# Decay by one power on GpSimd, a first mask from factor and triangle, stripe 1 on the whole array, and a new order of the list

## The chip, the cores and the metric

The kernel runs on one core of a Trainium2 chip. The core has five engines that run side by side and wait for one another by semaphores: TensorE (PE in the profile; its weight loads are PEld), VectorE (DVE), ScalarE (ACT), GpSimd (POOL) and SyncE (SP, which here only issues DMAs). Matmuls write to PSUM, eight banks of 128 partitions x 2 KB; everything else lies in SBUF. The metric is the device time of one execution in microseconds (us).

## The reference

Decayed linear attention over blocks of 64 positions (batch 4, 8 heads, 768 positions, head size 64), then an MLP with a quadratic, clipped activation. One block of the attention, for each batch and head:

```python
Dmask = np.where(rel >= 0, lam ** rel, 0.0)          # rel = i - j inside a block
intra = (q_b @ k_b.T * Dmask) @ v_b
inter = (q_b * lam ** (pos + 1)) @ kv_state
out_b = intra + inter
kv_state = lam ** 64 * kv_state + (k_b * lam ** (63 - pos)).T @ v_b
```

The outputs of all heads are laid side by side as x (3072 tokens x 512) and go through

```python
h = x @ w_in                                          # 512 -> 2048
g = where(h >= 1, h, where(h <= -1, 0, (h + 1) ** 2 / 4))
out = g @ w_out                                       # 2048 -> 512
```

## The kernel before, in words

The kernel works with blocks of 128 positions. The 24 blocks of the four batches are cut into eight stripes (`STRIPES`): stripe 0 has four blocks of batch 0, stripe 1 the two that are left of it, stripes 2 to 7 three each. A unit is a stripe and a pair of heads; stripe s has units s0 to s3. The MLP then runs on a whole stripe.

All order is written out by hand: `ORDER` is a list of words, each of which issues the instructions of one step, and every engine runs its own instructions in that order. The words of the attention, for unit 00 as an example: `L00k`, `L00q`, `L00v` load heads (SP issues them); `k00a`, `q02g`, `v01d` cast one to bf16, k and q times a power of lam, on ScalarE (a), VectorE (d) or GpSimd (g) (lines 275 to 311); `T00`, `Q00` transpose k and q on TensorE (334), `t00`, `u00` copy the transposes out on ScalarE (342, 344); `S00` is the scores (362), `s00` the mask on VectorE (371); `R00` the products k.T v (416, 422), `r00` the running state on VectorE (435, 444); `O00` the output (472 to 504), `o00` its copy into x on ScalarE (516). `z` spreads a cast k with zeros between the heads, for the form "f" (393, 395). Of the MLP: `K` is a part of the first three tiles of the up product for one quarter of x (575), `P` a whole tile of it (561), `h` its relu on ScalarE (584), `A` the rest of the activation on VectorE (541 to 543), `Y` a quarter of a down product (593), `y` its copy (601), `U` its store. `W0` to `W3` load quarters of w_in, `W4` to `W7` of w_out, as DMAs issued by GpSimd (232, 236); a word with `@` waits until the load named behind it has landed. `D1`, `D2` are one or two matmuls of a unit matrix whose result nobody reads (549, "warm-ups" below). `B` builds the masks of a pair of heads (216), `E` fills lam_z, the factors of stripe 0's scan (207), `J` zeroes the middle parts of the v and z tiles (260), `G` of other tiles.

`FORMS` says how each stripe's products of two heads stand in TensorE's array. "p": each head's 64 rows or columns in a half of its own, two matmuls side by side. "f": the whole array, with one head's data and zeros for the other, the state as a 128x128 block with zero corners. "w": outputs by token, transposes by DMA.

The powers of lam are made once: iota on GpSimd gives positions, ScalarE takes Ln(lam) (191), VectorE multiplies (194), ScalarE takes Exp (197); all later casts read `dec`. PSUM: four banks turn over for the MLP and the warm-ups (`pmm`), two for transposes, states and outputs (`pat`), two hold scores.

Of the kernel before, what the change touches and what calls it, by code (L numbers as in the profile page):

```python
# [23 lines left out]

FORMS = "ppffwwww"
STRIPES = [(0, 0, 4), (0, 4, 2), (1, 0, 3), (1, 3, 3), (2, 0, 3), (2, 3, 3), (3, 0, 3), (3, 3, 3)]

ORDER = """
L00k D1 D1 L01q D2 D2 D1 L02q L01k q01d k00a k01d D1 T00 q02g L00q q00d L01v L02k D1 D2 T01 t00
Q00 Q01 k02d v01a D1 B0a u00 S00 T02 D2 D1 B3a u01 L00v Q02 t01 L02v D2 E s00 S01 D2 L03q v02g
v00a L03k u02 D2 W0 D1 R00 q03g B1a L03v W2 D2 D2 B2a s01 W1@L00v L11q t02 W3 R01 r00 S02 r01
O00 v03g O01 o00 k03d D1 o01 T03 s02 L10v@W2 W4@L10v J Q03 t03 u03 R02 r02 S03 R03 O02 o02 D2
r03 s03 K00 L10q@W1 K02 O03 W5@L02k q11g K01 q12d q10g o03 K03 h02 P03 L10k@W2 h01 P08 q13g L11k
L11v k11g P0b h03 W6@L02q h00 P06 h08 h06 h0b P07 P04 P05 P09 W7@L00k h07 P0a Q12 h09 A00 Q10
k13d L20k@W5 h05 P0f h0a h04 k12d P0d u10 k10a P0e v13g T10 t10 T12 t12 P0c L20q u12 S10 L21k@W6
h0e D2 v10a h0f T11 T13 L20v Q13 A01 h0c Q11 Y030 u13 A02 s10 Y020 h0d t13 Y000 u11 Y010 t11  # L40
Y011 R10 v12a v11a r10 R11 S11 Y031 Y021 s11 Y001 S12 r11 R13 q21g O10 o10 Y022 Y032 A03 r13 s12
Y033 S13 R12 O11 Y012 y03 s13 r12 k20a o11 O13 k21a O12 q20d Y023 L21v@W1 o13 o12 z20a v21d P10
v20g y02 T20 T21 Q20 h10 P19 t21 P18 k23d Y002 L21q@W5 v22d Y013 q22g z21a t20 u20 h18 R20 P11
S20 k22d y01 h19 Q21 P13 h11 P12 u21 L31k q23d P16 L30k z22a Y003 T22 h13 h12 U02 P17 P15 L31q
h16 t22 r20 s20 y00 h17 A10 S21 Q22 k32d s21 P1a u22 Q23 T23 h1a R21 r21 L30q u23 P14 L30v v23g
z23g P1c P1f h15 k33g q30g P1d h14 P1b q31g S22 h1f h1c L31v O20 L40k t23 R23 k31a A11 o20 h1d
s22 P1e Y100 R22 Y110 k30a r23 z31g v32g r22 Y111 S23 O21 h1b L40q h1e Q30 T30 A12 s23 o21 A13
L40v Y101 u30 t30 O22 z30g T31 z32a o22 Y112 O23 v31d G40 v30g Y102 Q31 o23 S30 P22 s30 G42 R31
v33g u31 q32d t31 h22 P23 R30 Y113 P21 r30 h23 R32 G41 P29 q33d z33a y11 h21 r31 T32 Q32 P20 r32
k40d t32 u32 R33 r33 P2b h29 S31 P27 O30 q40g U03 h20 s31 h2b o30 S32 q42g Y103 Q33 T33 s32 t33  # L50
O31 P25 G43 h27 L50k u33 o31 T40 P26 P24 h26 h24 O32 S33 A20 P2c v40d q41d s33 h25 h2c U01 y10
k42a P2a O33 P28 o32 h28 k43g v41g P2d P2f T42 A21 P2e o33 k41d h2a q43d h2d G50 h2e R40 P32 P31
h2f R41 S40 A22 r41 h32 v42a P30 T41 A23 s40 P33 h31 h30 h33 Y200 P34 Y201 P36 L50v P37 T43 Y202
Y203 k51a L50q U11 L60k h37 h36 y20 P35 v43a P3a h3a r40 S41 O40 h34 A30 s41 P39 o40 v51d h39
R42 k50a P3b r42 P38 O41 U10 S42 P3f h35 h38 o41 P3e s42 q50a h3f X40 h3e O42 P3c q52d o42 A31
R43 v50d P3d h3b S43 r43 T50 q51d h3c Y210 Y220 v52g Y211 h3d k52a s43 Y212 R51 A32 X41 L60q
Y300 Y320 O43 Y321 U00 A33 Y322 X42 Y213 o43 X43 S50 y21 Y221 T51 Y301 Y323 y32 Y302 Y303 T52
P41 P40 R52 s50 r51 S51 R50 y30 P42 L60v Y222 q60a k53a k61d Y223 q53a q62g r50 h42 q61g k60g
s51 T53 h41 P43 h43 h40 P4b S52 T60 r52 U21 Y310 P46 h46 Y311 h4b s52 O52 P44 k62g O50 v61g o52
A40 h44 v53d k63g q63g v62a O51 U20 P48 T62 P4d Y312 S53 y22 T61 o50 h4d h48 v60a o51 P4c P49  # L60
h4c P47 R60 U30 s53 S60 h49 h47 s60 Y313 X50 L70k R53 r60 P45 S61 h45 y31 P4f X52 L70q O60 v63a
o60 P4a P4e X51 h4f h4a r53 Y410 Y400 A41 O53 o53 q71g Y420 h4e A42 Y411 R61 A43 U32 Y421 Y401
Y412 Y402 R62 X53 s61 Y413 P57 k72a Y403 h57 T63 L70v k70g r61 r62 y41 P51 h51 P5a S62 s62 P50
O61 y40 v73d Y422 R63 P53 k73a h50 o61 h53 S63 h5a s63 k71g q70g P52 U40 v72d P58 Y423 T71 O62
h52 y42 P59 P54 h59 h54 T70 P56 h56 P5b r63 P55 O63 A50 S70 h55 o62 o63 q73d s70 P5d R73 P5f h58
r73 R72 U41 X61 U22 P5e h5d h5b h5f v70a h5e U31 X62 P5c Y500 X63 A51 X60 A52 Y510 R70 h5c Y501
S71 Y511 P60 P63 h63 Y512 h60 Y502 A53 P68 q72g T73 r72 s71 Y503 Y513 P62 h68 v71g h62 T72 P61
y51 h61 S72 P67 R71 P6a P65 h67 h6a s72 r70 P6b h6b P66 U51 O72 y50 P69 A60 S73 r71 P6f o72 s73
h66 P64 X72 O71 h6f h69 P6d Y520 o71 Y521 h6d O70 P6c A62 o70 X71 h64 O73 Y522 h65 h6c P6e Y523
Y610 Y600 A61 o73 h6e A63 y52 X70 Y611 Y612 U42 Y601 Y602 X73 P75 Y613 Y603 y61 P78 P70 y60 h78  # L70
h75 P76 h76 P7b h7b P73 Y620 P71 U50 h73 h70 P72 U52 P7a U61 h71 P79 Y621 h72 h7a h79 Y622 A72
Y623 P74 h74 y62 P77 P7e h77 h7e P7d P7f A70 P7c h7d h7f h7c U60 Y710 A71 Y700 Y711 Y701 Y712
U62 A73 Y713 Y702 Y703 y71 y70 U71 U70 Z72
"""


# [5 lines left out]
def kernel(  # L82
# [64 lines left out]
    def load(s, n, which):  # L147
# [39 lines left out]
    one = const.tile([128, 1], F32, name="one")  # L187
    nc.vector.memset(one, 1.0)

    ln_lam = const.tile([128, H], F32, name="ln_lam")  # L190
    nc.scalar.activation(out=ln_lam, in_=lam_b, func=AF.Ln)
# [5 lines left out]
    nc.scalar.activation(out=dec, in_=ex, func=AF.Exp)
# [168 lines left out]
    def att_mask(u):  # L366

        s, hp = u
        C, T = shape(s)[:2]
        d = st[u]  # L370
        nc.vector.tensor_tensor(  # L371
            out=d["sc"][:, :, 0:C, :],
            in0=d["ps"][:, :, 0:T].rearrange("p h (c i) -> p h c i", c=C),
            in1=_ins(mask[:, 2 * hp:2 * hp + 2, :], 2, C), op=AX.mult)

    def before(u):

        s, hp = u
        C, T, first, last, fm = shape(s)
        if first:  # L380
            return None
        ss = st[s - 1, hp]["ss"]
        return ss[:, :, CM - 1] if s == 1 else ss[:, shape(s - 1)[0] - 1, :]

    def att_z(u, eng):
# [8 lines left out]
        else:  # L394
            (nc.gpsimd if eng == "g" else nc.vector).tensor_copy(dst, src)

    def att_r(u):

        s, hp = u
# [51 lines left out]
    def att_o(u):  # L451
# [180 lines left out]
    for word in order(NS):  # L632
# [73 lines left out]
```

## Time and profile before

| what | us |
|---|---|
| median of three runs (lowest, highest) | 226.18 (225.57, 227.38) |
| the profiled execution | 225.86 |
| its span in the profile | 224.1 |
| TensorE busy in the span | 214.2 |
| VectorE, ScalarE, GpSimd busy | 150.8, 128.8, 45.6 |

The profile is one execution, taken by the hardware. A group is named by line, engine, operation, output and input; its time in brackets is the idle time of its engine just before it and what ended that. The chain that ended last is followed back from the last instruction; a piece of it is what the end waited for at that time. The busy time of TensorE is modelled at the ends of its matmuls, so two neighbouring groups can overlap by a few hundredths of a microsecond.

### The profile page before, as it was taken

The numbers are of one execution on the slowest core, as the hardware profiler recorded it, in microseconds if no ns is written. First come the engines' busy times: TensorE is split into PE (matmuls) and PEld (weight loads), VectorE is DVE, ScalarE is ACT, GpSimd is POOL, SyncE is SP. The second block draws the span as 40 slices with busy tenths as digits, with TensorE's granted clock in tenths as the row PEclk, the third lists the DMA queues.
The fourth block names the chain that finished last, engine by engine and source line by source line (L and its number), as shares of the span: only waits on it lengthen the run. The fifth ranks groups of instructions, "written<-read, shape, count | busy, mean of one in ns | idle before, by whom it ended". The sixth has DMA issues, their size and how long they took to land.

```text
span 224.1 us, 4412 instructions
## 1 busy us (share of the span) xinstructions
PE 214.2 (96%) x1683; PEld 122.7 (55%) x1683; DVE 150.8 (67%) x236; ACT 128.8 (57%) x276; POOL 45.6 (20%) x90
## 2 busy tenths in 40 slices
PE   6498999999999999999999999999999999999994
PEld 1245544444776666656644666556665565455453
DVE  2547357885589888998894475993889486305930
ACT  5484277806886676958902766617682576074520
POOL 4453049002363442000102340061000000000000
PEclk9769999999999999999999999999999999999999
DMA  4999999998999992499899989899928104220112
GB/s 128 252 236 174 209 200 179 197 247 195 231 244 201 219 220 77 84 199 245 198 187 194 169 216 207 186 208 163 236 58 108 47 18 104 94 94 0 51 47 94
DMA packets 100629, 35.95 MB, mean 160 GB/s; under 512 B 89216, under 2 KB 97664, under 8 KB 100608
## 3 DMA queue, kind: packets, MB, share of 16 engines
q1 hardware_dynamic: 96384, 31.47, 65.6%
q0 software_dynamic: 4224, 4.19, 11.8%
q8 instruction: 13, 0.21, 0.4%
q14 instruction: 8, 0.07, 0.1%
HBM read 27.27 MB, written 6.29 MB: 150 GB/s over the span
## 4 chain that ended last, share of the span: by engine, by line
PE 87%; DVE 5%; DMA 2%; ACT 2%; SPq 2%; issue 1%; DVEq 0%; ACTq 0%
PE py L593 33%; PE ph L561 33%; PE pw L549 3%; PE pt L334 2%; PE ps L358 2%; DMA v_nat<-in_v_dram 2%; PE ps L362 2%; PE py L613 2%; PE pk L416 2%; DVE tt L542 1%; DVE gT L543 1%; PE po L472 1%; PE po L479 1%; PE ph L575 1%; SPq L162 1%; PE po L504 1%
## 5 line engine op out<-in xcount | busy, mean ns | idle before, releaser
L561 PE MATMUL ph<-xT,w_in_sb 128*128 128x384 bf16 (+2 forms) x500 | 90.9, 325 | 0.0
L584 ACT ACTIVATE tt<-ph,one 128x384 bf16<-128x384 f32 (+2 forms) x128 | 69.9, 592 | 32.5 <-PE ph L561 17.2
L593 PE MATMUL py<-w_out_sb,gT 128*128 128x512 bf16 x368 | 87.0, 379 | 0.3 <-DVE gT L543 0.3
L561 PEld LDWEIGHTS <-w_in_sb 128*128 128x128 bf16 x500 | 46.5, 98 | 28.8 <-issue 0.2
L593 PEld LDWEIGHTS <-gT 128*128 128x128 bf16 x368 | 34.5, 98 | 36.4 <-DVE gT L543 1.2
L371 DVE TENSOR_TENSOR sc<-ps,mask 128x768 bf16<-128x768 f32 (+2 forms) x32 | 30.5, 953 | 19.8 <-PE ps L358 14.2
L541 DVE TENSOR_SCALAR mm<-tt 128x1536 bf16<-128x1536 bf16 (+2 forms) x32 | 18.7, 583 | 21.8 <-ACT tt L584 20.8
L543 DVE TENSOR_TENSOR gT<-tt,mm 128x1536 bf16<-128x1536 bf16 (+2 forms) x32 | 31.7, 990 | 1.2
L542 DVE TENSOR_TENSOR tt<-tt,mm 128x1536 bf16<-128x1536 bf16 (+2 forms) x32 | 31.3, 979 | 1.1
L601 ACT COPY osb<-py 128x512 f32<-128x512 f32 x23 | 13.4, 584 | 23.3 <-PE py L593 23.3
L310 POOL TENSOR_TENSOR kq<-q_nat,dec 128x384 bf16<-128x384 f32 (+2 forms) x17 | 14.8, 890 | 48.4 <-DMA q_nat<-in_q_dram 35.6
L444 DVE SCALAR_TENSOR_TENSOR sz<-sz,lam_blk,pk 128x128 bf16<-128x128 bf16 x48 | 16.4, 346 | 1.7 <-PE pk L416 0.5
L287 POOL CAST vc<-v_nat 128x384 bf16<-128x384 f32 (+2 forms) x12 | 7.1, 588 | 48.1 <-PE po L498 31.5
L516 ACT CAST xT<-po 128x384 bf16<-128x384 f32 (+2 forms) x16 | 7.7, 481 | 15.3 <-PE po L504 11.7
L549 PE MATMUL pw<-ident 128*128 128x512 bf16 x31 | 11.5, 494 | 1.8 <-POOL ident masks.py:199 1.4
L334 PE MATMUL pt<-ident,kq 128*128 128x128 bf16 x96 | 9.8, 238 | 3.6 <-DVE kq L310 1.9
L310 DVE TENSOR_TENSOR kq<-k_nat,dec 128x384 bf16<-128x384 f32 (+2 forms) x11 | 7.5, 689 | 7.3 <-PE pk L416 4.6
L514 ACT CAST xn<-po 128x384 bf16<-128x384 f32 x16 | 7.7, 487 | 7.4 <-PE po L498 7.3
L334 PEld LDWEIGHTS <-kq 128*128 128x128 bf16 x96 | 7.1, 106 | 8.2 <-DVE kq L310 2.7
L301 ACT ACTIVATE kq<-k_nat,dec 128x192 bf16<-128x192 f32 (+2 forms) x26 | 10.6, 464 | 0.9 <-PE pk L416 0.9
L342 ACT COPY kqT<-pt 128x384 bf16<-128x384 bf16 (+2 forms) x16 | 7.7, 490 | 3.5 <-PE pt L334 3.5
L305 POOL TENSOR_SCALAR kq<-k_nat,dec 128x192 bf16<-128x192 f32 (+1 forms) x16 | 8.2, 528 | 2.9 <-PE pt L334 2.9
(74 smaller groups left out, 156.4 us busy)
## 6 DMA issues: line engine op xcount, KB each, us to landing
out_dram<-osb SPq DMA_DIRECT2D x23, 256.0 KB, 2.4
q_nat<-in_q_dram SPq DMA_DIRECT2D x18, 256.0 KB, 4.3
k_nat<-in_k_dram SPq DMA_DIRECT2D x24, 128.0 KB, 4.3
v_nat<-in_v_dram SPq DMA_DIRECT2D x24, 128.0 KB, 4.0
k_nat<-in_k_dram SPq DMA_DIRECT2D x12, 256.0 KB, 4.9
v_nat<-in_v_dram SPq DMA_DIRECT2D x12, 256.0 KB, 4.8
w_in_sb<-in_moe_w_in_dram POOLq DMA_DIRECT2D x4, 512.0 KB, 9.3
w_out_sb<-in_moe_w_out_dram POOLq DMA_DIRECT2D x4, 512.0 KB, 7.6
```

Source lines behind the costliest of these rows:

```text
L310: (nc.gpsimd if eng == "g" else nc.vector).tensor_tensor(dst, src, decay(row, 2 * hp, C, inner), op=AX.mult)
L334: nc.tensor.transpose(out=d["pt"][:, i, c, :], in_=d["kq"][:, i * C + c, :], identity=ident)
L371: nc.vector.tensor_tensor(out=d["sc"][:, :, 0:C, :], in0=d["ps"][:, :, 0:T].rearrange("p h (c i) -> p h c i", c=C), in1=_ins(mask[:, 2 * h ...
L444: nc.vector.scalar_tensor_tensor(out=d["ss"][:, c, :], in0=prev, scalar=lam_blk[:, hp:hp + 1], in1=kv, op0=AX.mult, op1=AX.add)
L541: nc.vector.tensor_scalar(mm, tt, 0.5, 1.0, AX.mult, AX.min)
L542: nc.vector.tensor_tensor(tt, tt, mm, op=AX.subtract)
L543: nc.vector.tensor_tensor(g[:, 4 * a:4 * a + 4, 0:T], tt, mm, op=AX.mult)
L549: nc.tensor.matmul(pw, lhsT=ident, rhs=_ins(ident[:, :], 1, 4), start=True, stop=True)
L561: nc.tensor.matmul(ph[:, 0:T], lhsT=w_in_sb[:, ko, ni * 128:(ni + 1) * 128], rhs=x_tiles[s][:, ko, 0:T], start=(ko == 0), stop=(ko == KO - 1))
L584: nc.scalar.activation(out=t_tiles[s, ni // 4][:, ni % 4, 0:T], in_=p_tiles[s, ni][:, 0:T], func=AF.Relu, bias=one[:, 0:1])
L593: nc.tensor.matmul(y_tiles[s, m], lhsT=g_tiles[s][:, ko, m * 128:(m + 1) * 128], rhs=w_out_sb[:, ko, :], start=(ko == 0), stop=(ko == FO - 1))
L601: nc.scalar.copy(out=osb, in_=y_tiles[s, m])
```

## The change

Four things. First, `dec` is one instruction on GpSimd, `tensor_tensor` with the operation pow, base lam and exponent position; Ln, the product and Exp go, and lam_z is zeroed behind the power instead of ahead of it. Second, for stripe 0 the mask is applied as (score x factor) x triangle, by one VectorE instruction per head, so it needs `dec` and the triangle and no mask built by `B`. Third, stripe 1 has form "f": its k is spread by `z`, the state that it takes over from stripe 0 is copied into a 128x128 tile with zero corners by the new word `b`, and four such tiles are zeroed in `J`. Fourth, the list is another one from its start to the middle of stripe 6; the last 309 words are the same. There are 31 warm-ups in both lists. The switches PK_PAT and PO_PAT stand as before the change (all in `pat`).

```diff
-FORMS = "ppffwwww"
+FORMS = "pfffwwww"
 ORDER = """
-L00k D1 D1 L01q D2 D2 D1 L02q L01k q01d k00a k01d D1 T00 q02g L00q q00d L01v L02k D1 D2 T01 t00
-Q00 Q01 k02d v01a D1 B0a u00 S00 T02 D2 D1 B3a u01 L00v Q02 t01 L02v D2 E s00 S01 D2 L03q v02g
-v00a L03k u02 D2 W0 D1 R00 q03g B1a L03v W2 D2 D2 B2a s01 W1@L00v L11q t02 W3 R01 r00 S02 r01
-O00 v03g O01 o00 k03d D1 o01 T03 s02 L10v@W2 W4@L10v J Q03 t03 u03 R02 r02 S03 R03 O02 o02 D2
-r03 s03 K00 L10q@W1 K02 O03 W5@L02k q11g K01 q12d q10g o03 K03 h02 P03 L10k@W2 h01 P08 q13g L11k
...
+L00q D2 E B2a D1 D2 D1 L02k q00d D2 B0a D2 L00k k00g L01v k02d T02 D2 T00 t00 Q00 L01k L02q k01a
+q02d u00 L00v L03q D2 Q02 T01 v00a L01q S00 s00 q01g t02 L03v q03d u02 L03k D2 D2 R00 r00 W0 D1
+L02v v01d Q01 W1 t01 u01 v03d D2 D2 k03g W2@L00v Q03 S01 O00 v02g D2 L10q u03 T03 o00 D1 L11q
+R01 L10v@W1 s01 S02 r01 s02 O01 B1a t03 R02 o01 r02 S03 R03 O02 r03 K01 q10g K00 s03 o02 O03 o03
+K02 Q10 P03 L10k L11k q11d h03 Q11 K03 h00 P07 h01 P06 h02 h06 P05 W3@L01v J W4@L10v P0b P09
...
-    ln_lam = const.tile([128, H], F32, name="ln_lam")
-    nc.scalar.activation(out=ln_lam, in_=lam_b, func=AF.Ln)
-    ex = const.tile([128, NR, H], F32, name="ex")
-    pa, la = pos[:, :], ln_lam[:, :]
-    nc.vector.tensor_tensor(
-        ex, bass.AP(pa.tensor, pa.offset, list(pa.ap) + [[0, H]]), _ins(la, 1, NR), op=AX.mult)
     dec = const.tile([128, NR, H], F32, name="dec")
-    nc.scalar.activation(out=dec, in_=ex, func=AF.Exp)
+    pa = pos[:, :]
+    nc.gpsimd.tensor_tensor(
+        dec, _ins(lam_b[:, :], 1, NR), bass.AP(pa.tensor, pa.offset, list(pa.ap) + [[0, H]]),
+        op=AX.pow)
...
+    corners = [const.tile([128, 128], BF16, name=f"bd{i}") for i in range(NP if FORMS[1] == "f" else 0)]
...
+        for t in corners:
+            nc.gpsimd.memset(t, 0.0)
...
+        if s == 0 and STT:
+            for hi in range(2):
+                nc.vector.scalar_tensor_tensor(
+                    out=d["sc"][:, hi, 0:C, :],
+                    in0=d["ps"][:, hi, 0:T].rearrange("p (c i) -> p c i", c=C),
+                    scalar=dec[:, 2, 2 * hp + hi:2 * hp + hi + 1],
+                    in1=_ins(causal[:, :], 1, C), op0=AX.mult, op1=AX.mult)
+            return
...
+        if fm == "f" and FORMS[s - 1] == "p":
+            return corners[hp]
...
+    def att_b(u, eng):
+
+        s, hp = u
+        ss = st[s - 1, hp]["ss"]
+        last = ss[:, :, CM - 1] if s == 1 else ss[:, shape(s - 1)[0] - 1, :]
+        for hi in range(2):
+            p0 = hi * D
+            o = corners[hp][p0:p0 + D, p0:p0 + D]
+            if eng == "a":
+                nc.scalar.copy(out=o, in_=last[p0:p0 + D])
+            else:
+                (nc.gpsimd if eng == "g" else nc.vector).tensor_copy(o, last[p0:p0 + D])
```

More of the change, by code (lines that the diff above doesn't have):

```diff
@@ L37 @@
-r03 s03 K00 L10q@W1 K02 O03 W5@L02k q11g K01 q12d q10g o03 K03 h02 P03 L10k@W2 h01 P08 q13g L11k
[L38 to L72, printed above, removed]
@@ L73 @@
-U62 A73 Y713 Y702 Y703 y71 y70 U71 U70 Z72
+L00q D2 E B2a D1 D2 D1 L02k q00d D2 B0a D2 L00k k00g L01v k02d T02 D2 T00 t00 Q00 L01k L02q k01a
[3 more added lines that the diff above has]
+K02 Q10 P03 L10k L11k q11d h03 Q11 K03 h00 P07 h01 P06 h02 h06 P05 W3@L01v J W4@L10v P0b P09
@@ new lines @@
+L11v u10 v11g k11g h07 A00 W5@L01k q12d P0a B3a h05 L20k@W5 h0b P08 k12g W6@L01v q13d h09 u11
+k10a P0e h0e k13d z11g T10 P04 t10 T11 P0c h04 S10 t11 h08 P0d Q13 v10d W7@L03k L21k@W6 h0c T13
+Q12 s10 z10d S11 t13 D1 P0f u13 b10a R10 L20q b11g T12 z12a h0a v12g Y010 t12 A01 h0d Y020 L20v
+b13g h0f Y000 Y030 L21q@W6 r10 O10 v13a k20a Y031 A02 Y001 o10 Y021 b12g Y002 Y022 A03 Y011 k23g
+Y023 Y003 R11 u12 s11 R12 Y012 S12 k22d z13d r12 R13 z20g Y032 s12 y02 r13 z22a S13 s13 r11 D1
+O12 k21g q20d L30q o12 y00 Y033 v20d O13 O11 Y013 o11 L21v Q20 T20 o13 P10 v21g q21d y03 P11 Q21
@@ new lines @@
+t20 u20 P17 R20 S20 h11 L30k q22g y01 P1b P13 r20 T21 s20 L31k h17 P12 z21d h10 h13 L31q u21 P16
+q23d P1a q31g v23g O20 h12 U02 P14 t21 L30v T22 h1b Q22 P15 o20 k31g L31v h16 t22 u22 S21 D1 Q23
+z23d P18 A10 h15 s21 h14 R21 h1a T23 P1c P19 t23 r21 v22g P1e A11 L40k S22 h1c u23 T31 P1f h18
+h19 k30a O21 P1d Q31 t31 o21 Y100 s22 Y101 u31 q30d S23 h1e R22 T30 Y110 A12 h1f L40q t30 s23
+Q30 Y102 v30g u30 R23 k32a r22 q33g S30 r23 D1 z30g O22 Y111 o22 R30 h1d A13 O23 Y112 q32g s30
+o23 z31a z32a P20 T32 G42 v32g v31d k33d h20 P2b Q32 t32 h2b Y103 S31 u32 G40 G41 r30 D1 Y113
@@ new lines @@
+y11 U03 L50k R31 P23 P22 h23 L40v h22 s31 R32 P21 v33g h21 r31 G43 z33g T33 S32 Q33 k42d q42a
+P25 t33 r32 P29 s32 A20 h25 P27 R33 y10 u33 P26 h26 P2a k41a O30 h27 P24 h2a S33 q40a L50q P28
+q41g r33 h24 U10 P2c o30 k40d h29 h28 O31 P2e k43d o31 s33 h2c P2d P2f q43a h2f A21 v41g G50
+v43a O32 T40 o32 O33 o33 T41 Y200 h2d A22 Y201 h2e P33 P3a R41 R43 P31 A23 h3a v42a q50g k50g
+h31 P32 r41 h32 r43 Y202 P30 Y203 h33 S40 R42 P37 h30 P39 s40 r42 A30 q52a h39 T43 U00 P36 S41
+h37 h36 P35 P34 s41 P38 T42 T50 y20 h34 Y210 h35 P3d A31 h38 h3d L50v S42 P3f v40g P3c P3b h3f
@@ new lines @@
+R40 L60q L60k s42 P3e O41 q51g o41 h3b r40 U01 Y211 S43 k53a h3c O40 k51g O42 Y300 k52g Y301 o42
+Y320 h3e v50a s43 O43 A32 X42 U11 Y321 o40 Y212 X40 X41 v51g S50 Y213 o43 X43 T52 T51 R51 Y220
+L60v Y221 A33 Y302 Y322 v52a y21 s50 Y303 r51 Y323 P42 Y222 R50 q53d y32 y30 P41 S51 R52 Y223
+q60a P40 r50 q62a k61d h42 k60a T53 s51 h41 P43 h43 h40 P4b S52 T60 r52 U21 Y310 P46 h46 Y311
+h4b s52 O52 q61g P44 k62g O50 v61g o52 A40 h44 v53d k63g q63g v62a O51 U20 P48 T62 P4d Y312 S53
+y22 T61 o50 h4d h48 v60a o51 P4c P49 h4c P47 R60 U30 s53 S60 h49 h47 s60 Y313 X50 L70k R53 r60
@@ new lines @@
+P45 S61 h45 y31 P4f X52 L70q O60 v63a o60 P4a P4e X51 h4f h4a r53 Y410 Y400 A41 O53 o53 q71g
+Y420 h4e A42 Y411 R61 A43 U32 Y421 Y401 Y412 Y402 R62 X53 s61 Y413 P57 k72a Y403 h57 T63 L70v
+k70g r61 r62 y41 P51 h51 P5a S62 s62 P50 O61 y40 v73d Y422 R63 P53 k73a h50 o61 h53 S63 h5a s63
+k71g q70g P52 U40 v72d P58 Y423 T71 O62 h52 y42 P59 P54 h59 h54 T70 P56 h56 P5b r63 P55 O63 A50
+S70 h55 o62 o63 q73d s70 P5d R73 P5f h58 r73 R72 U41 X61 U22 P5e h5d h5b h5f v70a h5e U31 X62
+P5c Y500 X63 A51 X60 A52 Y510 R70 h5c Y501 S71 Y511 P60 P63 h63 Y512 h60 Y502 A53 P68 q72g T73
@@ new lines @@
+r72 s71 Y503 Y513 P62 h68 v71g h62 T72 P61 y51 h61 S72 P67 R71 P6a P65 h67 h6a s72 r70 P6b h6b
+P66 U51 O72 y50 P69 A60 S73 r71 P6f o72 s73 h66 P64 X72 O71 h6f h69 P6d Y520 o71 Y521 h6d O70
+P6c A62 o70 X71 h64 O73 Y522 h65 h6c P6e Y523 Y610 Y600 A61 o73 h6e A63 y52 X70 Y611 Y612 U42
+Y601 Y602 X73 P75 Y613 Y603 y61 P78 P70 y60 h78 h75 P76 h76 P7b h7b P73 Y620 P71 U50 h73 h70 P72
+U52 P7a U61 h71 P79 Y621 h72 h7a h79 Y622 A72 Y623 P74 h74 y62 P77 P7e h77 h7e P7d P7f A70 P7c
+h7d h7f h7c U60 Y710 A71 Y700 Y711 Y701 Y712 U62 A73 Y713 Y702 Y703 y71 y70 U71 U70 Z72
@@ L108 @@
     NK = 3
+    STT = True
+    PK_PAT, PO_PAT = (1, 1, 1, 1), (1, 1, 1, 1)
     NKZ = 4 if "f" in FORMS else 0
@@ L266, with bank @@
     st = {}
+    def bank(pool, name):
+        n = CM * (D if name == "pk" else BLK)
+        return pool.tile([128, 512], F32, name=name, tag="pat" if pool is pat else "pmm")[:, 0:n]
     def decay(row, h0, C, inner):
@@ L406, in att_r @@
         elif s == 0:
-            d["pk"] = pk = pat.tile([128, D, CM], F32, name="pk", tag="pat")
+            d["pk"] = pk = bank(pat if PK_PAT[hp] else pmm, "pk").rearrange("p (e c) -> p e c", c=CM)
             d["ss"] = ssp.tile([128, D, CM], BF16, name="ss", tag="ss")
@@ L467, in att_o @@
         else:
-            d["po"] = po = pat.tile([128, CM, 128], F32, name="po", tag="pat")
+            d["po"] = po = bank(pmm if s == 0 and not PO_PAT[hp] else pat, "po").rearrange(
+                "p (c i) -> p c i", c=CM)
         for c in range(C):
@@ L653 @@
             set_middles()
+        elif f == "b":
+            att_b((n[0], n[1]), word[3])
         elif f == "z":
```

## The prediction

> **What bounds the kernel now.** I read the page first. TensorE is busy for 214.2 of 224.1 us, and its row of tenths is low only in the first slices and in the last, at full clock from slice 4 on.
>
> ```profile
> PE 214.2 (96%) x1683; PEld 122.7 (55%) x1683; DVE 150.8 (67%) x236; ACT 128.8 (57%) x276; POOL 45.6 (20%) x90
> ...
> PE   6498999999999999999999999999999999999994
> ...
> PEclk9769999999999999999999999999999999999999
> ```
>
> Then the chain that ended last. Its tail after 203.6 us is VectorE's last gates and the last products; the list of the change is the same there word for word. From 24 to 90 us only two stretches of it are not TensorE: 38.55 to 40.13 (ScalarE, 1.58 us) and 78.38 to 80.77 (VectorE, 2.39 us). From 90 to 203 us TensorE has no wait worth naming. So a change of the list's first part can win only in the head (before the first product P03 of stripe 0, at 27.60), up to 4.0 us in the two stretches, and in the matmuls themselves. The head's chain:
>
> ```profile
> 5.47 4.56 DMA v_nat<-in_v_dram
> ...
> 10.10 0.62 ACT vc L285
> 10.72 0.60 ACT mask L216 x2
> 11.32 0.48 ACT kqT L344
> ...
> 11.84 0.61 PE ps L362 x8
> ...
> 27.60 7.84 PE ph L561 x36
> ```
>
> Columns are start, length, what. A load and three ScalarE pieces decide when the first scores start (11.84); from there TensorE is dense to 27.6, warm-up matmuls (L549) among it. The timeline gives the steps that the change touches:
>
> ```profile
> 3.76 0.21 ACT L191 ACTIVATE ln_lam<-lam_b 128x8 f32<-128x8 f32 x1 [1.67 <-DMA lam_b<-in_lam_dram]
> 3.99 1.28 ACT L197 ACT_TABLE_LOAD   x1
> ...
> 5.28 0.29 ACT L197 ACTIVATE dec<-ex 128x104 f32<-128x104 f32 x1
> ...
> 7.18 1.06 POOL L310 TENSOR_TENSOR kq<-q_nat,dec 128x512 bf16<-128x512 f32 x1 [3.90 <-DMA q_nat<-in_q_dram]
> 8.18 1.33 POOL L207 COPY lam_z<-lam_blk 128x768 f32<-128x768 f32 x1
> ...
> 15.99 1.22 DVE L371 TENSOR_TENSOR sc<-ps,mask 128x1024 bf16<-128x1024 f32 x1 [2.21 <-ACT mask L216]
> ```
>
> The decay is ready at 5.57, and a mask kept VectorE idle for 2.21 us. Last, the busy time by stretch, cut where the granted clock (after the five engines) changes:
>
> ```profile
> 5.17:8.59 3.42, 1.04 (x7) 0.43 (x7) 1.47 (x4) 1.88 (x5) 1.41 (x2) 1.00 1.06 280
> 8.59:12.00 3.41, 2.23 (x17) 1.49 (x19) 2.07 (x3) 1.90 (x6) 0.93 (x1) 0.50 1.16 225
> 12.00:15.41 3.41, 3.41 (x21) 1.61 (x17) 1.23 (x2) 2.54 (x7) 1.92 (x3) 0.50 1.12 249
> 15.41:18.82 3.41, 3.41 (x40) 1.62 (x41) 1.97 (x3) 1.55 (x5) 3.41 (x5) 1.00 1.15 196
> ```
>
> The first number after the width is TensorE's busy time. A stretch busy 1.04 or 2.23 us is followed by half clock, one busy throughout by full clock.
>
> **The power.** Gone: Ln 0.21, Exp 0.29 and one table load 1.28 on ScalarE, the 0.27 product on VectorE. New: one power of 128x104 on GpSimd from 3.77, when lam has landed (positions are ready at 3.31). No row shows a power. GpSimd's products take 0.709, 0.907 and 1.062 us for 256, 384 and 512 elements: about 0.36 plus 1.4 ns per element, so one pass of 104 costs 0.50, the lower end. If it works like many passes inside one instruction, 20 of them cost 0.36 + 20 x 0.145 = 3.3 us, my upper end (an estimate). I take 1.0, nearer the rows; the decay is then ready at 4.8 instead of 5.57. The Trainium skill ("GPSIMD Engine Reference", Performance versus the Vector engine) says that bodies of three or more operations go at about three operations per cycle; by that, 36 operations would be about 1.0 us. No run here shows it.
>
> Behind the power on GpSimd stand, in order, the memset of lam_z (0.95; until now done while lam was on its way), its fill (1.33) and the cast k00 (two of about 0.69, by 0.362 for 128 and 0.552 for 192). The first two end at 4.8 + 2.3 = 7.1. The loads are issued one after another and land about 1.05 us apart per 256 KB piece (second at 6.3, sixth at 10.03, seventh about 11.3); k00 is now third and lands at 7.1. So the power has until 4.8 (a length of about 1.05) for nothing; beyond that every microsecond delays k00, T00 and S00.
>
> **The new head, walked by rows.** Pieces land: q00 4.9, k02 6.2, k00 7.1, v01 8.1, k01 9.3, q02 10.0, v00 11.3, q03 12.3, q01 13.2, v03 14.2, k03 15.4, v02 16.4. Copies are 0.59 alone, 0.5 back to back; matmul groups are the chain's, doubled at half clock. k00 cast 7.1 to 8.45, T00 8.9, t00 9.5, k01 cast 10.4, u00 11.0, Q02 and T01 11.75, S00 11.75 to 12.35 (before: 11.84 to 12.45, so no gain yet). v00 cast 11.9, t02 and u02 12.9; four warm-ups to 14.05, R00 14.5, warm-up 14.9, Q01 15.3 (its cast needs q01: 13.2 + 1.06), four warm-ups at full clock 16.3, Q03, S01 16.9.
>
> The mask of stripe 0 no longer waits for ScalarE: two instructions with a factor and the triangle. Nearest rows for one: 0.688 (128x512 product with a mask), or half of 1.22; I take 0.65, so 1.3 per unit against 1.22. VectorE: s00 12.4 to 13.7, q03 14.4, state 15.2, v01 and v03 casts 16.4, s01 16.95 to 18.25, r01 19.5 (R01 waits for o00 and two masks on ScalarE), s02 20.8, r02 21.5, r03 22.2, s03 23.5. TensorE: O00 17.55, T03 18.25, R01 18.8, O01 20.2, R03 21.5, O02 22.2, K01 and K00 23.5, O03 24.15, K02 24.8, Q10, **P03 at 24.95**. The six K matmuls of K03 (0.65) now come after P03, the Q10 (0.2) before it, so 25.4 answers to 27.60: about 2.0 us won (27.44 is its record, 27.60 the chain's), mostly because 12 warm-ups stand after S00 instead of 17 and T02 and Q02 stand before it. The w_in quarter that K01 needs is issued at 14.1, as now at 14.03, and landed 7.2 us later: 21.3, or 0.5 later with one more q load beside it; it is not late for 22.2.
>
> **Stripe 1 on the whole array.** Before, the four state-and-output groups of it take 0.52, 0.52, 0.49 and 0.49 us with 0.18 of products ahead of the last two: 2.2. The new form has two matmuls at 0.03 and six at 0.056 each: 0.40 per unit, 1.6 in all; 0.6 us of TensorE saved. Five warm-ups stand after K00 instead of two: 3 x 0.216 = 0.65 at most, nothing where they fill a wait; I take 0.3. The added spreads (z: 0.4 to 0.5 us by the 128x384 row of 0.525), corner copies and memsets go to GpSimd (20% busy), ScalarE and VectorE beside TensorE; VectorE gets about 2 us more between 24 and 60, where it idles some 40%. The state in 128 columns costs 0.346 against 0.274. If that cover were gone they would cost 2 us.
>
> **Given back.** TensorE reaches the first down products about 2.5 us sooner (38.3 against 41.17), but they need w_out's quarters, whose first issue hangs behind v of stripe 1, which hangs behind a w_in quarter, as now (30.97 issued, 7.5 landing): 37.8, then by the present spacing 40.4, 43.9, 47.0, for use at 38.3, 42.1, 44.7, 47.3. The margins are 0.5 to 1.7. ScalarE has 16 rectified tiles at 0.6 and some 4.6 us of copies from 26 on, so 40 is its own end. I take 0.4 lost.
>
> Sum: -2.0 - 0.6 + 0.3 + 0.4 = -1.9 on the profiled run's 225.86 (span 224.1 and 1.8 around it): 223.96. The median shown, 226.18, is 0.3 above that run, so **224.3**.
>
> **Rivals.** (1) The power is long. Place: GpSimd's queue ahead of k00. From 1.05 us on it costs one for one; and once S00 starts after about 12.9, the stretch 12.00 to 15.41 is no longer full and the clock stays at half until 18.82, about 1.2 us more. It eats the gain at some 2.2 us; at 4 us the time is 224.3 + 2.95 + 1.2 = 228.5. For: nothing shows a power; against: GpSimd's other rows are short. Chance 0.22. That clock rule is in the Trainium skill ("TensorE: Matmul & The Clock Gate", Part 1): windows of 3.413 us that run freely, half clock by default and full after a busy one. The stretches above agree (3.41 us), and by a shifted window the same head would also move. The skill also speaks against the change ("GPSIMD Engine Reference", Instruction dispatch): the first call of a freshly loaded GpSimd library loads code for about 6 us unseen. No GpSimd instruction of this trace shows such a gap; by it the time would pass 229, and I give it 0.03 of the 0.22.
>
> (2) All is given back: w_out's quarters or ScalarE hold the first down products where they were, and the head's 2.0 turns into a wait around 38 to 47 us: 225.3 to 226.5. The margins of half a microsecond speak for it. 0.20.
>
> (3) The new list also closes the 1.58 and 2.39 us stretches: 222 to 223. The warm-ups put in there speak for waits that stay. 0.13. (4) The power is no shorter than what it replaces and changes nothing: S00 is set by v00, k01 and copies anyway; then the time is the forecast's, since the gain is elsewhere.
>
> **How the numbers follow.** Forecast 0.45, spread 223.2 to 225.3. Faster by over 1% (below 223.9; 1% is what a measurement here can tell from no change) is rival 3 and two fifths of the forecast: 0.31, with 0.02 for longer savings 0.33. Slower by over 1% (over 228.4) is three quarters of rival 1: 0.17. Between: 0.50. The range 222.4 to 228.4 leaves out the deep end of (3) and the long end of (1); a power of 3.3 us lies inside.
>
> **What would show it.** The power's row and its length; k00's cast starting at its load; S00 near 11.8 and P03 near 25; no mask wait ahead of s01; half clock ending at 15.4; the non-TensorE pieces of the chain near 38 to 47 and 78. Wrong if the power is over 2 us, if full clock comes a stretch later, or if a quarter of w_out ends a wait.

## The result

| | before | after |
|---|---|---|
| median (lowest, highest), us | 226.05 (225.57, 227.38), 4 runs | 240.49 (240.46, 240.49), 4 runs |
| ratio after / before, 95% interval | | 1.063 (1.058 to 1.067) |
| the profiled execution, us | 225.86 | 240.49 |
| its span, us | 224.1 | 238.8 |
| decay ready at | 5.57 | 21.02 |
| first product P03 of stripe 0 (its record) | 27.44 | 42.36 |
| from there to the end of the span | 196.7 | 196.4 |

The kernel became 14.4 us slower: all of it is lost before P03, and nothing behind it. The page of the changed kernel, busy time first, then rows of tenths (each digit is a slice of 5.97 us), then one of its costliest groups:

```profile
PE 212.0 (89%) x1653; PEld 123.4 (52%) x1675; DVE 152.3 (64%) x239; ACT 127.2 (53%) x273; POOL 73.8 (31%) x113
...
PE   6000898999999999999999999999999999999994
...
POOL 6999970950724216037022022008000000000000
PEclk9655589999999999999999999999999999999999
...
L194 POOL TENSOR_TENSOR dec<-lam_b,pos 128x104 f32<-128x104 f32 x1 | 17.0, 16983 | 1.6 <-DMA lam_b<-in_lam_dram 1.6
```

TensorE did about the same work (212.0 against 214.2 us busy; 22 records of matmuls are missing in the changed kernel's trace), but it has three empty slices at the start, and in just these slices GpSimd is full. The group says with what: one instruction, the power, of 16.98 us. The head of the chain that ended last (start, length, what):

```profile
0.81 3.08 DMA lam_b<-in_lam_dram
...
4.03 16.99 POOL dec L194
...
21.96 0.17 DVE lam_blk L199
...
22.16 1.93 DVE kq L316 x2
...
24.13 0.61 PE pt L340 x4
```

Before, a load of v and ScalarE's copies decided this part; now the chain is lam's load, then the power, then the first casts that read `dec`, then the first transpose at 24.13 (before: 6.56). The waits show that everything stood behind one instruction (total, times, longest):

```profile
PE pt L340 <- DVE kq L316: 19.1, 1, 19.1
ACT mask L215 <- POOL dec L194: 19.0, 1, 19.0
DVE lam_blk L198 <- POOL dec L194: 18.6, 1, 18.6
```

And the timeline right behind the power:

```profile
20.98 0.94 POOL L201 MEMSET lam_z<- 128x1024 f32 x1
21.05 0.90 DVE L198 COPY lam_blk<-dec 64x4 f32<-64x4 f32 x1 [18.62 <-POOL dec L194]
```

The copy of 64x4 elements takes 0.90 us here and 0.161 before. It lies beside the memset of lam_z, which the change put behind the power, and the two end within 0.03 us of each other. That is a small second loss, on the chain.

### The profile page after: what moved, and what is told of

Its sections match the earlier page's. It is cut to its first block, busy times and chain, and to the rows that moved or that the text cites. A ratio compares the mean times of both kernels' runs of the same rounds, so it can differ in the third digit from the quotient of the medians.

```text
span 238.8 us, 4394 instructions
## 1 busy us (share of the span) xinstructions
PE 212.0 (89%) x1653; PEld 123.4 (52%) x1675; DVE 152.3 (64%) x239; ACT 127.2 (53%) x273; POOL 73.8 (31%) x113
## 4 chain that ended last, share of the span: by engine, by line
PE 80%; DVE 8%; POOL 7%; issue 1%; DMA 1%; ACT 1%; DVEq 0%; ACTq 0%; POOLq 0%
PE ph L591 31%; PE py L623 31%; POOL dec L194 7%; PE pt L340 3%; PE ps L364 2%; PE pw L579 2%; PE ps L368 2%; DVE tt L572 2%; PE pk L445 2%; PE po L502 2%; PE py L643 1%; DMA lam_b<-in_lam_dram 1%; DVE gT L573 1%; PE po L509 1%; PE ph L605 1%
## 5 line engine op out<-in xcount | busy, mean ns | idle before, releaser
L614 ACT ACTIVATE tt<-ph,one 128x384 bf16<-128x384 f32 (+2 forms) x128 | 70.8, 588 | 32.4 <-PE ph L591 20.0
L623 PE MATMUL py<-w_out_sb,gT 128*128 128x512 bf16 x348 | 85.3, 379 | 1.3 <-DVE gT L573 0.3
L385 DVE TENSOR_TENSOR sc<-ps,mask 128x768 bf16<-128x768 f32 (+1 forms) x28 | 25.6, 915 | 18.7 <-PE ps L364 14.7
L340 PE MATMUL pt<-ident,kq 128*128 128x128 bf16 x96 | 10.9, 238 | 19.8 <-DVE kq L316 19.1
L311 POOL TENSOR_SCALAR kq<-k_nat,dec 128x192 bf16<-128x192 f32 (+2 forms) x28 | 15.6, 569 | 31.6 <-PE pk L445 12.1
L316 POOL TENSOR_TENSOR kq<-q_nat,dec 128x384 bf16<-128x384 f32 (+2 forms) x14 | 12.9, 925 | 20.8 <-ACT kq L307 16.9
L194 POOL TENSOR_TENSOR dec<-lam_b,pos 128x104 f32<-128x104 f32 x1 | 17.0, 16983 | 1.6 <-DMA lam_b<-in_lam_dram 1.6
L293 POOL CAST vc<-v_nat 128x384 bf16<-128x384 f32 (+2 forms) x14 | 8.1, 579 | 30.2 <-DMA v_nat<-in_v_dram 11.4
L198 DVE COPY lam_blk<-dec 64x4 f32<-64x4 f32 x1 | 0.9, 900 | 18.6 <-POOL dec L194 18.6
L215 ACT ACTIVATE mask<-causal,dec 128x128 f32<-128x128 f32 x8 | 2.7, 395 | 19.0 <-POOL dec L194 19.0
```

Source lines behind the costliest of these rows:

```text
L194: nc.gpsimd.tensor_tensor(dec, _ins(lam_b[:, :], 1, NR), bass.AP(pa.tensor, pa.offset, list(pa.ap) + [[0, H]]), op=AX.pow)
L311: nc.gpsimd.tensor_scalar(dst[:, hi, :, :], src[:, hi, :, :], dec[:, row, 2 * hp + hi:2 * hp + hi + 1], 0.0, AX.mult, AX.add)
L340: nc.tensor.transpose(out=d["pt"][:, i, c, :], in_=d["kq"][:, i * C + c, :], identity=ident)
L385: nc.vector.tensor_tensor(out=d["sc"][:, :, 0:C, :], in0=d["ps"][:, :, 0:T].rearrange("p h (c i) -> p h c i", c=C), in1=_ins(mask[:, 2 * h ...
L614: nc.scalar.activation(out=t_tiles[s, ni // 4][:, ni % 4, 0:T], in_=p_tiles[s, ni][:, 0:T], func=AF.Relu, bias=one[:, 0:1])
L623: nc.tensor.matmul(y_tiles[s, m], lhsT=g_tiles[s][:, ko, m * 128:(m + 1) * 128], rhs=w_out_sb[:, ko, :], start=(ko == 0), stop=(ko == FO - 1))
```

## Experiments

The theory after the result was that the power alone costs the 14 us and some 2 more, and that the rest of the change is worth about what the prediction said. The rivals: that the new list itself is also late (a clock that stays low, loads out of step), and that the power's length is a fixed price of a first call, or hangs on the exponents, so that another place or size would mend it.

### The changed kernel without the power (e1_lnexp), and the old one with it (e2_before_pow)

The edit of e1_lnexp, made in the changed kernel; e2_before_pow is the reverse of it, made in the kernel before.

```diff
+    ln_lam = const.tile([128, H], F32, name="ln_lam")
+    nc.scalar.activation(out=ln_lam, in_=lam_b, func=AF.Ln)
+    ex = const.tile([128, NR, H], F32, name="ex")
+    pa, la = pos[:, :], ln_lam[:, :]
+    nc.vector.tensor_tensor(
+        ex, bass.AP(pa.tensor, pa.offset, list(pa.ap) + [[0, H]]), _ins(la, 1, NR), op=AX.mult)
-    pa = pos[:, :]
-    nc.gpsimd.tensor_tensor(
-        dec, _ins(lam_b[:, :], 1, NR), bass.AP(pa.tensor, pa.offset, list(pa.ap) + [[0, H]]),
-        op=AX.pow)
+    nc.scalar.activation(out=dec, in_=ex, func=AF.Exp)
```

> The changed kernel with the decay made as before (Ln, product, Exp) and all else of the change kept. Theory A, the power alone made the loss: in the changed kernel's trace the decay is ready at 21.02 instead of 5.57, 15.45 us later, and P03 starts at 42.52; with the decay at 5.6 the walk of the prediction holds again and P03 starts near 25 to 26, so 240.5 - 16.5 to 17.5 = 223 to 224, faster than before by 1%. Rival B, the other parts also cost (list, form, mask) and the late decay only hid it, because every load had landed by then: 227 or more. Rival C, they give nothing: within 0.5 us of 226.05.

Measured: 224.41 us (224.30 to 224.49), 0.991 of before (0.989 to 0.993; before here 226.34). That is 0.4 above the upper end of theory A and far from the rivals. So list, form and mask together win 1.9 us, and the power turns that into a loss: 240.49 - 224.41 = 16.1 us.

> The kernel before with only the decay made by one power on GpSimd. Theory A: the power takes 17 us here too and everything behind it starts 15.4 us later, less what waits for loads cost in the head before: 239 to 241.5. Rival B (the new queue order on GpSimd makes the power dear, or the other parts cost much): under 235.

Measured: 241.06 us in one run, 14.7 over before. The power took 16.984 us there as well, in another list and between other instructions. So the power alone makes the loss in the old list too. It is 1.4 us less than the 16.1 of the new list; what makes up this difference isn't shown.

The head of e1_lnexp in its chain of waits:

```profile
5.42 0.30 ACT dec L199
...
6.12 1.93 DVE kq L319 x2
...
8.09 0.61 PE pt L343 x4
...
12.95 0.54 PE ps L371 x6
...
25.85 0.86 PE ph L594 x4
```

The decay ends at 5.72, the first transpose starts 2.4 us later, the scores S00 at 12.88 by their record and P03 at 25.69. In the changed kernel the same steps are decay 21.02, transpose 3.1 us later, P03 at 42.36. The later decay accounts for 15.3 of the 16.7 us by which P03 is later; 0.7 is the slow copy of lam_blk with what hangs on it; the last 0.6 lies between the transpose and P03, where its chain has two casts of v on VectorE (2.38 us from 32.47) that e1_lnexp's has not, and where half clock lasts for 7.3 us behind the first transpose instead of 6.3; the two aren't told apart. Behind P03 the changed kernel is 0.5 us quicker (196.4 against 196.9); why isn't shown.

### What the power costs by size (e3_split)

```diff
-    nc.gpsimd.tensor_tensor(
-        dec, _ins(lam_b[:, :], 1, NR), bass.AP(pa.tensor, pa.offset, list(pa.ap) + [[0, H]]),
-        op=AX.pow)
+    for r0, r1 in ((0, 1), (1, 3), (3, NR)):
+        nc.gpsimd.tensor_tensor(
+            dec[:, r0:r1, :], _ins(lam_b[:, :], 1, r1 - r0),
+            bass.AP(pa.tensor, pa.offset + r0, [list(pa.ap)[0], [1, r1 - r0], [0, H]]),
+            op=AX.pow)
```

> The changed kernel with the power cut in three instructions on the same queue: 8, 16 and 80 elements per partition. Theory A1, a price per element (16.98 us / 104 = 163 ns): about 1.3, 2.6 and 13.1 us, the kernel at 240 to 241. Rival A2, a fixed price paid once (code brought in at the first call): the first about 16, the others under 1 us, the kernel at 240 to 241. Rival A3, the price grows with the exponent: the second, all exponents 128 and -128, costs over 300 ns per element, and the third less than 163.

Measured: 240.12 us in one run. Its three groups on GpSimd, with busy time and mean ns of one:

```profile
L195 POOL TENSOR_TENSOR dec<-lam_b,pos 128x80 f32<-128x80 f32 x1 | 13.1, 13100 | 0.0
...
L195 POOL TENSOR_TENSOR dec<-lam_b,pos 128x16 f32<-128x16 f32 x1 | 2.9, 2888 | 0.0
...
L195 POOL TENSOR_TENSOR dec<-lam_b,pos 128x8 f32<-128x8 f32 x1 | 1.7, 1680 | 1.6 <-DMA lam_b<-in_lam_dram 1.6
```

From 8 to 16 elements a partition: (2888 - 1680) / 8 = 151 ns each; from 16 to 80: 160; from 80 to the 104 of the changed kernel: 162. A straight line, with 0.4 us where it meets zero. So it is a price by element, about 160 ns, and no fixed price: the first call of the program, the one of 8 elements, takes 1.68 us in all. The size of the exponent does not matter to it either, for the lam of these inputs (0.97 to 0.99): the 16 elements hold the rows of 128 and -128, and lie on the line. Splitting the instruction leaves the time nearly where it was (240.12 against 240.49), and in the other list it is as long; on GpSimd only fewer elements make it shorter. A power on another engine was not run.

### A shorter power (e8_pow24)

```diff
+    nc.vector.memset(dec[:, 3:NR, :], 1.0)
     nc.gpsimd.tensor_tensor(
-        dec, _ins(lam_b[:, :], 1, NR), bass.AP(pa.tensor, pa.offset, list(pa.ap) + [[0, H]]),
-        op=AX.pow)
+        dec[:, 0:3, :], _ins(lam_b[:, :], 1, 3),
+        bass.AP(pa.tensor, pa.offset, [list(pa.ap)[0], [1, 3], [0, H]]), op=AX.pow)
```

> The changed kernel with the power for three of the 13 rows (24 elements) alone; the other rows are set to 1, so q is not decayed rightly: that part of the computation is left out. By e3's lengths the power takes 0.4 + 24 x 0.16 = 4.2 us and the decay is ready near 8.3, against 5.71 in e1. The prediction's rival 1 (one for one behind GpSimd's queue and about 1.2 us more for a later full clock): 224.4 + 2.6 + 0.9 of lam_z's zeroing, which now comes behind, + 1.2 = 229.1 or so, 228 to 229.5. Other theory, the loads hide part: 226 to 227.5.

The kernel leaves out the power for ten of the 13 rows, which stay at 1. Measured: 227.58 us in one run, between the two expectations. The power takes 4.20 us, the decay is ready at 8.21 (2.5 later than in e1_lnexp), S00 at 16.15 (3.3 later), P03 at 29.40 (3.7 later), the whole 3.2 later. The stretches, cut as in the prediction (TensorE busy first, then PEld, VectorE, ScalarE, GpSimd, the granted clock, DMA share, GB/s):

```profile
8.59:12.00 3.41, 0.69 (x5) 0.56 (x6) 3.22 (x5) 0.92 (x4) 3.06 (x3) 0.50 0.94 265
12.00:15.41 3.41, 2.74 (x15) 1.39 (x14) 0.00 (x0) 2.13 (x5) 2.54 (x4) 0.50 1.04 242
15.41:18.82 3.41, 3.41 (x28) 1.63 (x26) 2.02 (x3) 1.33 (x3) 3.36 (x7) 0.52 1.05 220
18.82:22.24 3.42, 3.34 (x45) 2.08 (x40) 2.93 (x6) 2.10 (x4) 3.42 (x10) 1.00 1.21 196
```

The clock stays at half until 18.7, as rival 1 said it would for a power of this length: the stretch 12.00 to 15.41 is busy 2.74 of 3.41, and half clock follows. (That gives no threshold: in e10_best the stretch from 8.02 to 11.43 us is busy for 2.74 us too, and full clock follows.) But the price is smaller than the 1.2 us put down for it. P03 is 3.7 us late where the decay is 2.5 late, but 0.7 of this difference is there at the first transpose already (11.31 against 8.09; the copy of lam_blk takes 0.90 us here too). So at most 0.5 is left for the clock, and about 0.5 of the delay comes back behind P03. Between e1_lnexp and this run each microsecond of decay costs 3.2 / 2.5 = 1.27; so the 1.9 us that the rest wins would be eaten by a decay 1.5 us later than in e1_lnexp, a power of some 3.2 us. This is an estimate from two kernels, one of them run once; a power of that length has 17 elements by the line above, where the kernel needs 104.

### The list, the form and the mask apart (e9_list, e6_nostt, e5_lnexp_formp)

All three keep Ln and Exp. e6_nostt has the new list and form with the old mask; e9_list is e6_nostt with stripe 1 in the old form, so the new list alone; e5_lnexp_formp is e1_lnexp with the old form.

The edit of e6_nostt in e1_lnexp; in the list, besides, B1a moves ahead of t02 and B3a behind R02, so that the masks are there in time:

```diff
-    STT = True
+    STT = False
```

The edit of e9_list in e6_nostt, and of e5_lnexp_formp in e1_lnexp; the words z10 to z13 and b10 to b13 leave the list:

```diff
-FORMS = "pfffwwww"
+FORMS = "ppffwwww"
```

> As e1, and the first mask as before (one product per unit with a mask that ScalarE builds; the masks of units 1 and 3 moved ahead of their first use). In e1 the two instructions with factor and triangle take 0.742 us each, 1.48 per unit, against 1.22 for the one product, and VectorE is on the chain in the head (s01 to s03). Theory, the new mask's gain is only the wait that it removes, and the list's early masks remove it as well: this is 0 to 0.8 us faster than e1 (3 x 0.26 at most). Rival, ScalarE's four masks in the head now hold its copies: 0.5 to 1.5 us slower than e1.

Measured: 223.66 us (223.29 to 224.18), 0.990 of before (0.986 to 0.994; before here 226.09). The interval overlaps with that of e1_lnexp: with the two masks moved, the new form of the mask is worth nothing that can be measured. In e1_lnexp one such instruction takes 0.740 us, so a unit 1.48 against 1.22 for the product with the mask.

> The new list alone: as e6 with stripe 1 in the old form too, so decay, mask and form are those of the kernel before. Theory, the list (fewer warm-ups behind the first scores, loads in another order) is what wins the head, and the form wins 1.25 us (e5 against e1): 225.0 to 225.8. Rival, the list wins nothing without form and mask: 226.0 to 226.8.

Measured: 225.10 us (224.34 to 226.26), 0.996 of before (0.994 to 0.9985). The list alone wins about 1.0 us.

> As e1, and stripe 1 in the form of before (two products side by side; the words z1 and b1 taken out of the list, no corner tiles). Theory: the whole array saves 0.6 us of TensorE's time and costs little beside it, so this is 0.3 to 1.0 us slower than e1. Rival: the spreads and corner copies cost more than is saved: this is faster than e1 by 0.5 us or more.

Measured: 225.66 us (225.01 to 227.03), 0.997 of before (0.994 to 1.000), 1.25 over e1_lnexp; e9_list is 1.4 over e6_nostt. The form is worth more than the 0.6 put down for it (the 0.3 set against that was for warm-ups, which stand in all four kernels). Where it wins can be read from the time behind P03 in the profiled runs:

| kernel | form of stripe 1 | P03 | from P03 to the end |
|---|---|---|---|
| e1_lnexp | f | 25.69 | 196.9 |
| e6_nostt | f | 25.06 | 196.9 |
| e5_lnexp_formp | p | 26.00 | 198.0 |
| e9_list | p | 24.57 | 198.0 |

With each form the two agree, and the forms differ by 1.1 us. It is time in which TensorE works: behind P03 it is busy for 193.3 us in e1_lnexp and for 194.5 in e5_lnexp_formp, and in neither does one of its waits there reach 0.4 us. (Only these two can be compared so; in the traces of the other two 22 records of matmuls are missing.) The counted products are 0.6 us of it; which others make up the rest stays open.

The table also shows that P03 itself lies up to 1.4 us apart in kernels with one list and nearly one decay. The section after this one shows what most of it goes with.

### A decay sooner by another way (e7_series, e11_before_series, e10_best)

The power was meant to spare ScalarE's Ln, a table load and Exp. Here VectorE makes Ln from four terms of its series in lam - 1 (lam is near 1 in these inputs), and Exp stays. The edit is made in e1_lnexp for e7_series, in the kernel before for e11_before_series and in e6_nostt for e10_best:

```diff
-    nc.scalar.activation(out=ln_lam, in_=lam_b, func=AF.Ln)
+    um = const.tile([128, H], F32, name="um")
+    nc.vector.tensor_scalar(um, lam_b, 1.0, None, AX.subtract)
+    nc.vector.tensor_scalar(ln_lam, um, -0.25, 1.0 / 3.0, AX.mult, AX.add)
+    nc.vector.tensor_tensor(ln_lam, ln_lam, um, op=AX.mult)
+    for c in (-0.5, 1.0):
+        nc.vector.scalar_tensor_tensor(out=ln_lam, in0=ln_lam, scalar=c, in1=um, op0=AX.add, op1=AX.mult)
```

> As e1, with Ln(lam) taken by four terms of the series in lam - 1 on VectorE (good for lam near 1, here 0.97 to 0.99), so that ScalarE loads only Exp's table, early: the load of 1.28 us behind Ln goes, and five small VectorE steps of some 0.06 to 0.2 us come in: the decay near 5.0 instead of 5.71. Theory, the decay is still on the path in e1 (the chain goes through it, then VectorE's casts): 0.3 to 0.7 us faster than e1. Rival, the loads decide (k02 lands at 6.2, k00 at 7.1): within 0.2 us of e1.

Measured: 223.98 us (223.37 to 225.02), 0.991 of before (0.988 to 0.994), not to be told from e1_lnexp. In its profile the decay is ready at 5.50 instead of 5.71, S00 starts at 11.98 instead of 12.88 and P03 at 24.70 instead of 25.69. Only 0.2 of this is the decay. Nearly all the rest goes with the clock: from the start of the first transpose to the end of T00 it is 1.89 us in e1_lnexp and 1.21 in e7_series, as the two warm-ups between them show (e1_lnexp, then e7_series):

```profile
8.49 1.06 PE L582 MATMUL pw<-ident 128*128 128x512 bf16 x2
...
8.12 0.59 PE L587 MATMUL pw<-ident 128*128 128x512 bf16 x2
```

In e1_lnexp the granted clock is at half from 7.6 to 14.4 us, in e7_series only from 9.6 to 13.0. With the same list e5_lnexp_formp has 6.8 us of half clock too, and P03 at 26.00; e9_list has 3.4, and P03 at 24.57. So P03 moves by about 1 us with the length of the half clock, under one list and nearly one decay, and a single profile of a head has to be read with that. The timeline of e7_series also shows the next thing late:

```profile
22.09 1.24 PE L613 MATMUL ph<-xT,w_in_sb 128*128 128x512 bf16 x5 [0.47 <-DMA w_in_sb<-in_moe_w_in_dram]
```

The first part of the up product waits 0.47 us for its quarter of w_in. e9_list, whose P03 is as early, shows the same wait at 0.35 us. Both waits lie ahead of P03.

> The kernel before with the series in place of Ln and nothing else. In its trace the chain to the first scores goes through the load of v (10.03), not through the decay. Theory: no difference, within 0.5 us of before. Rival, an earlier decay brings the first casts and the clock forward: 0.5 to 1 us faster.

Measured: 226.33 us (225.35 to 226.75), 1.000 of before (0.999 to 1.0015). In the old list a shorter way to the decay changes nothing that can be measured. In its profile the decay is ready at 5.04 instead of 5.57, but the first scores start only 0.2 us sooner (11.62), as rival 4 of the prediction has it. P03 is at 26.70 instead of 27.44; behind it TensorE waits 1.2 us for a cast on GpSimd (at 36.03), and the span is none the shorter (224.6).

> e6 and e7 together: the new list, stripe 1 on the whole array, the mask as before, the decay by series and Exp. Theory, the two small gains of e6 (0.6 us of span against e1) and e7 (0.9 us) add as long as no load waits: 223.0 to 223.6, ratio near 0.987. Rival, the first quarter of w_in, for which e7's first K already waited 0.47 us, bounds the head and the two don't add: 223.6 to 224.2.

Measured: 224.53 us (223.86 to 225.83), 0.993 of before (0.991 to 0.996), so above both expectations and not better than either of its parts. The profiled run took 225.59, 1.1 us above the median, so its profile need not stand for the others. Its chain of waits, between 19 and 52 us, is no longer TensorE's:

```profile
19.24 0.76 POOL w_in_sb L244
...
32.18 0.71 POOL w_out_sb L248
...
35.89 9.19 DMA w_out_sb<-in_moe_w_out_dram
...
45.52 2.19 SPq L171
...
47.75 3.79 DMA k_nat<-in_k_dram
```

The third quarter of w_out is issued at 35.89 and lands at 45.08; SyncE's loads of a later stripe, which the list lets wait for it, start only then, and k lands at 51.53, when VectorE casts it. In this run the first part of the up product had also waited 1.40 us for w_in. This shows the place; that it costs the whole 0.9 us between e10_best and e6_nostt isn't shown, since the two were run beside different runs of the kernel before and their intervals touch.

The best of these kernels are e1_lnexp, e6_nostt and e7_series: about 0.99 of the time before, with no measurable difference among them. All leave the power away.

## Why the prediction was wrong

**The step that failed is the price of the power.** It was put at 1.0 us, with "20 of them cost 0.36 + 20 x 0.145 = 3.3 us, my upper end". It took 16.98 us, five times the upper end. The start, 0.4 us, was right; the price by element was not: 160 ns against 1.4 ns of a product, a factor of about 110. The upper end was no bound at all. It was a guess at the number of passes, worked out from rows of another kind of work, one arithmetic pass, and nothing in the trace limits how long a function takes that no row shows. The rule that was set beside it, in the Trainium skill ("GPSIMD Engine Reference", Performance versus the Vector engine), gives an estimate of about 1.0 us for some 36 operations at three per cycle; the measurement decides against its use here. The same page (Instruction dispatch) puts about 6 us on the first call of a freshly loaded library; no run here shows that: in e3_split the first power, of 8 elements, took 1.68 us and lies on the line, and it began at 4.03, 0.14 us after lam had landed.

**The mechanism behind it was right, as rival 1.** GpSimd's queue ahead of k00, one for one from about 1 us on: its own sum for the measured length is 224.3 + (16.98 - 1.05) + 1.2 = 241.4, against 240.49. In e8_pow24 the sum would be 228.65, and the time is 227.58; so it is about 1 us too long both times. One reason is the clock term, at most 0.5 instead of 1.2 in e8_pow24. Another can be the point from which it counts: e1_lnexp reaches the forecast with a decay at 5.71, while the sum lets nothing behind 4.8 pass free. Its chance of 0.22 and the range up to 228.4 came from the upper end of 3.3 and fell with it.

**Without the power the number held, and partly by luck.** The forecast of 224.3 stands beside 224.41 (e1_lnexp), but by the profiled runs the head gave 1.3 us instead of 2.0 (27.44 less 0.45, against 25.69), the form 1.1 instead of 0.6, and 0.85 was lost behind the head instead of 0.7. These errors nearly cancel (1.55 us in all instead of 1.9), and the 0.3 that the forecast added for the median makes up the rest. By its parts:

- The head. P03 was put at 24.95 with a decay at 4.8; it is 25.69 with a decay at 5.71 (e1_lnexp). The walk has no time for the cast k02, which takes 1.31 us and ends at 8.04. T00, which stands behind T02 and two warm-ups, then ends at 9.98 instead of 8.9, and S00 starts at 12.88, not at 11.75. Half clock lasts as long as the prediction has it, but from 7.6 to 14.4 instead of 8.59 to 15.41 (granted 0.65 in 12.00 to 15.41). That it ends 1 us sooner can be why P03 is late by less than S00.
- The mask. The wait of 2.21 us for ScalarE's mask is gone (s01 waits 0.48 us for TensorE's scores), but e6_nostt shows that this form isn't what wins: with masks built a little sooner the old product does as well. One instruction takes 0.74, not 0.65.
- Stripe 1's form. The sign was right, the size not: 1.25 and 1.4 us in two pairs of kernels, against 0.6. (The 0.3 beside it was for the list's warm-ups.)
- Given back. With the form of before, the new list takes 198.0 us behind P03 (e5_lnexp_formp, e9_list), 1.3 more than before. Of this 0.45 are the products that moved behind P03, so 0.85 is lost. Five warm-ups stand there instead of two, and TensorE has no idle time in which the three more could be free (busy for 63.97 of the 64 us from 26 to 90 in e5_lnexp_formp): at the prediction's 0.216 each that is 0.65, an estimate. So the term taken at 0.3 is its full 0.65, and the loads, taken at 0.4, cost little there: none of TensorE's waits behind P03 in these two traces is for a load. The loads were met ahead of P03 instead, by 0.35 and 0.47 us of waiting for w_in in e9_list and e7_series and by 1.40 in e10_best. (The walk's 37.8 for the first quarter of w_out does not follow from its 30.97 + 7.5, which is 38.5; in e1_lnexp the first down product starts at 39.44 and waits for no load.)
- The stretches at 38.55 and 78.38 us (rival 3). In e1_lnexp TensorE is busy throughout from 38 to 41 and from 76 to 82 us (3.00 and 6.00 us by the stretches). Yet its time behind P03 is the old one within 0.3 us. There was less to win than the "up to 4.0 us": the pieces of the chain there are not TensorE's, but in the kernel before it was busy for 3.45 of these 3.97 us, with matmuls off the chain.
- Rival 4, that S00 isn't set by the decay, is true in the kernel before (e11_before_series). In the new list the decay is on the chain (e1_lnexp), but a decay 0.2 us sooner moved no measurable time (e7_series).

## What to carry to other kernels

A price for an operation that no row of the trace shows can't be bounded by rows of other operations; time it alone, at two sizes, before it is put anywhere. Least of all is it put at the start, where the first value that all engines read has nothing to hide it: there an error in the price is paid one for one. And a gain in the head is to be read together with the time behind it: with the form of before, the new list's head was 1.0 and 2.4 us shorter in two profiled runs (with 6.8 and 3.4 us of half clock), and the median of e9_list won 1.0, since 0.85 was lost behind the head. A head that starts sooner also meets the loads of the weights, here by 0.35 to 1.40 us of waiting.

## What was not expected of the hardware

- GpSimd's power of two f32 operands takes 0.4 us plus about 160 ns for each element of a partition (1.68, 2.89, 4.20, 13.10 and 16.98 us for 8, 16, 24, 80 and 104), also for the rows of largest exponent, and 16.983 and 16.984 us in two different kernels.
- The power does not hold up a small copy on VectorE. In e3_split lam_blk is copied while the third power runs (8.6 to 21.6 us), in 0.28 and 0.17 us:

```profile
8.61 0.28 DVE L200 COPY lam_blk<-dec 64x4 f32<-64x4 f32 x1 [6.19 <-POOL dec L195]
8.91 0.17 DVE L201 COPY lam_blk<-dec 64x4 f32<-64x4 f32 x1
```

- Other work of GpSimd does hold up VectorE. The same copy takes 0.90 us where it starts just behind the memset of lam_z (the changed kernel, e2_before_pow, e8_pow24), and 0.161 without it. The 128x512 product for k02 takes 1.31 us where it starts during the fill of lam_z (the changed kernel, e1_lnexp, e8_pow24), and 0.69 alone; but in the kernel before a product that starts at 8.14, 0.04 us ahead of the fill, takes 0.69 with the fill beside it. For the 128x10 step of the positions the rows give no rule: beside the same memset it takes 1.14 us in two traces (before, e5_lnexp_formp) and 0.25 in six. The Trainium skill ("GPSIMD Engine Reference", Specifications) says that GpSimd shares its interfaces to SBUF with VectorE, with contention where the VectorE instruction has two inputs in SBUF or runs in a 2-port mode. The product has two inputs, and its rows agree; the copy has one, and no trace shows its mode.
